# Attention, layer norm and a two-layer MLP on one core: another order for the first batch, and the second weight matrix loaded by rows

## The chip, the core and the metric

The kernel runs on one core of a Trainium2 chip. A core has five engines with instruction streams of their own: TensorE (PE) for matrix products and transposes, VectorE (DVE), ScalarE (ACT) for exponentials and other functions, GpSimd (POOL) for elementwise work, and SyncE (SP), which here only issues DMAs. DMAs are issued from the queues of SP, POOL and, at the very start, ACT. The metric is the device time of one execution in microseconds (us).

## What is computed

Eight batches with 12 heads, 448 positions and a head size of 64. Cut to what matters, the reference is

```python
q_n, k_n = rmsnorm(q, g_q), rmsnorm(k, g_k)          # over the 64 of a head
scores = (1 / 8) * q_n @ k_n^T
attn = softmax(scores)
x = (attn @ v) with the heads side by side           # 8 x 448 x 768
xn = (x - mean) / sqrt(var + 1e-6) * g_ln
out = x + relu(xn @ w_ch1) @ w_ch2                   # 768 -> 3072 -> 768
```

Inputs and output are float32; the products run in float16 with float32 sums. The first weight matrix (W1) is 768 x 3072, the second (W2) 3072 x 768. Both stay in SBUF from their load on.

## The kernel before

**Units and pairs.** Two heads make a pair, six pairs a batch. Loads and preparation go by units: the first batch has four units (one, one, two and two pairs), every later batch three units of two pairs. So units 0 to 3 are batch 0 and hold pairs 0 to 5, units 4 to 6 are batch 1, and unit 7 is the first of batch 2. For a unit, `pieces` gives the steps by a letter each: `b` takes the loaded tiles, `a` squares k and `c` squares q, `d` and `e` sum those squares, `g` (or `gk` and `gq` apart) takes the inverse root, `i` multiplies k by the product of the two gains, `j` casts k to float16 and `k` subtracts the cast from k (k is kept as a high and a low float16 part), `l` scales q, `m` doubles it, `z` brings the values.

**Which engine does what.** Some steps have tables of units that say which engine takes them: `DVE_KG` (step `i` on VectorE instead of GpSimd), `POOL_HI` (`j` on GpSimd instead of ScalarE), `POOL_DUP` (`m` on GpSimd instead of VectorE), `POOL_SQUARE` (`a` as (unit, 1) and `c` as (unit, 0) on GpSimd instead of ScalarE), `POOL_LO` (`k` on GpSimd instead of VectorE). `ACT_Q` lists the pairs whose transposed q ScalarE, not VectorE, copies from PSUM to SBUF.

**The hand-written list.** `ORDER` is a list of tokens that covers batch 0's attention, the first pair of batch 1, the normalisation of batch 0's result and the start of its first layer. `first_attention` walks it and emits each token's instructions. Every engine runs its own instructions in the order of the list, and waits only where data or buffers demand it. `K` and `Q` transpose a pair's k and q on TensorE, through PSUM, with a copy to SBUF. `Sp.i` is score block i of pair p on TensorE and the exponential of it on ScalarE; two PSUM banks take the scores in turn. `Vp.i` multiplies the exponentials with the values; after block 6, VectorE divides by the sums. `T`, `A`, `N`, `X` and `R` are the normalisation (sums, their combination, the normalised rows, their transposes, the root), `U` the first three blocks of the first layer. `L` loads a unit's inputs, `W` a third of W1, `G` the layer norm's gain. `H` and `J` with a number are fillers: that many 128-column products (`H`, L532) or transposes (`J`, L535) whose results nobody reads.

**After the list.** `run_rest` emits the MLP of each batch in chunks (L798 and L821 for the later batches, L718 and L728 for the first) and between them the attention steps of the next batch from a list that `attention` plans; a step is emitted when the MLP's estimated work has come as far as the step's share. TensorE's stream is thus an interleaving of both. Unit 7 is the first whose k and q are transposed by DMAs (`dma_k`, L306; `dma_q`, L312) issued from SP.

**W2.** `load_w2(0)` is emitted at step 47 of that plan, `load_w2(1)` at step 71, both on GpSimd's queue (L616). The DMAs convert float32 to float16. Before the second call stands a one-element cast on GpSimd (L613) that reads the transposed k of unit 7, so the call waits for that DMA transpose. Today the first call brings the left 384 columns of all 3072 rows with one DMA, the second the right 384 columns with two, of 1536 rows each. The MLP of batch 0 (`first_mlp`) has 21 chunks of the first layer and then 24 of the second (psC, L728): three tiles of 128 positions (t), two halves of the columns (g), four quarters of the 3072 rows, with six products of 128 rows each in a chunk. It runs column half by column half, in that tile by tile, in that quarter by quarter, so that one PSUM bank at a time collects a tile's 24 products before VectorE adds them (L757). The pool for these banks, `ps_m`, has three.

Of the kernel before, what the change touches and what calls it, by code (L numbers as in the profile page):

```python
# [8 lines left out]
FP32 = mybir.dt.float32  # L9
# [7 lines left out]
ts = bass.ts  # L17
# [3 lines left out]
NDC, NFF = DM // 128, FF // 128  # L21
# [3 lines left out]
PAIR_UNIT = [(u, w) for u, (_, _, m) in enumerate(UNITS) for w in range(m)]  # L25
UNIT_PAIR = [PAIR_UNIT.index((u, 0)) for u in range(len(UNITS))]
EXP_BIAS = -4.0
DVE_KG, POOL_HI, POOL_DUP, ACT_Q = (0, 6), (1, 2, 3, 4, 5, 6, *range(8, 25)), (3, 4, 5, 6), (0, 2, 4, 5)
POOL_SQUARE, POOL_LO = ((2, 1), (4, 0), (6, 0)), (5, 6)

# [1 line left out]


ORDER = """
b0 H12 a0 L4 c0 i0 e0 j0 H24 b1 gq0 d0 k0 l0 a1 m0 K0 G gk0 i1 H10 L5 c1 Q0 d1 j1 S0.0 b2 S0.1
H5 a2 e1 g1 S0.2 c2 S0.3 k1 l1 z0 d2 e2 m1 K1 S0.4 i2 H16 S0.5 S0.6 Q1 g2 H5 J8 b3 l2 j2 k2 c3
V0.0 S1.0 z2 S1.1 S1.2 V1.0 J8 a3 m2 H4 V0.1 z3 S1.3 K2 S1.4 V0.2 Q2 V0.3 V0.4 d3 S1.5 V0.5 V0.6
S2.0 S1.6 V1.1 V1.2 S2.1 e3 W0 i3 K3 V2.0 S2.2 V2.1 S2.3 Q3 j3 T0 S2.4 k3 V1.3 g3 V1.4 S2.5 S2.6  # L40
l3 b4 V1.5 m3 c4 S3.0 S3.1 V2.2 S3.2 K4 a4 V1.6 S3.3 V2.3 S3.4 Q4 d4 V2.4 V2.5 V3.0 V3.1 V3.2
V2.6 i4 S3.5 j4 J4 S3.6 V3.3 T1 K5 e4 k4 S4.0 W1 S4.1 S4.2 Q5 z4 b5 S4.3 V3.4 V4.0 V3.5 S4.4
V4.1 V4.2 S4.5 W2 V4.3 S5.0 g4 V3.6 S4.6 S5.1 J4 V5.0 V4.4 G2 S5.2 l4 T3 K6 V4.5 V5.1 V4.6 S5.3
T4 V5.2 a5 L6 V5.3 S5.4 m4 Q6 i5 S5.5 V5.4 S5.6 V5.5 V5.6 T5 S6.0 S6.1 J4 S6.2 A V6.0 S6.3 V6.1
N0 N1 S6.4 S6.5 J4 V6.2 X0 V6.3 d5 j5 N2 S6.6 V6.4 X1 z5 Q7 c5 V6.5 R U0 e5 U1 g5 X2 V6.6 M k5
U2 K7 b6 L7 a6 L8k c6 i6 l5 m5 e6 d6
""".split()
DMA_UNIT = 7
PE_SET = (DMA_UNIT + 1) % 2
# [16 lines left out]
HALF, HCOL = NFF // 2, DM // 2  # L66
# [25 lines left out]
class _Fast:  # L92
# [518 lines left out]
    def load_w2(self, g):  # L611
        if g:
            self.nc.gpsimd.tensor_copy(out=self.rr[:, DMA_UNIT:DMA_UNIT + 1],  # L613
                                       in_=self.kU[DMA_UNIT % 2][:, 0:1])
        for c in (slice(0, HALF), slice(HALF, NFF)) if g else (slice(0, NFF),):
            self.nc.gpsimd.dma_start(  # L616
                out=self.sh.w2[:, c, ts(g, 384)],
                in_=self.w2[128 * c.start:128 * c.stop, ts(g, 384)].rearrange("(c p) d -> p c d", p=128))

    def tok_tiles(self, b):  # L620
        x = self.xs[b]
# [86 lines left out]
    def first_mlp(self):  # L708

        nc, sh = self.nc, self.sh  # L710
        tiles, xnT, hT, cur = self.tok_tiles(0), self.xnT, self.hS, {}

        def up(f, i):
            if i == 0:
                cur["h"] = self.ps_m.tile([128, 512], FP32, tag="mlp", name="psH")
            ps = cur["h"]
            for dc in range(3 * i, 3 * i + 3):
                nc.tensor.matmul(ps[:, 0:384], sh.w1[:, dc, ts(f, 128)], xnT[:, dc],  # L718
                                 start=(dc == 0), stop=(dc == NDC - 1))
            if i:  # L720
                nc.scalar.activation(out=hT[:, f], in_=ps[:, 0:384], func=AFT.Relu)

        def down(t, g, s):
            if s == 0:
                cur["ps"] = self.ps_m.tile([128, 512], FP32, tag="mlp", name="psC")
            ps = cur["ps"][:, 0:HCOL]
            for f in range(3 * s, 3 * s + 3):
                nc.tensor.matmul(ps, hT[:, f, ts(t, 128)], sh.w2[:, f, ts(g, HCOL)],  # L728
                                 start=(f == 0), stop=(f == NFF - 1))
            if s == 7:  # L730
                self.add(0, t, g, ps)
                if g and t < 2:
                    self.late.append((0, t, slice(0, DM)))
                elif t == 2 and not g:
                    self.late.append((0, t, slice(0, HCOL)))
                elif t == 2:
                    self.store(0, t, slice(HCOL, DM))
            elif s == 3:
                self.store_late()

        for f in range(UP_FIRST, NFF):
            yield 6 * 384 / 2.4, [lambda f=f, i=i: up(f, i) for i in range(2)]
        for g in range(2):
            for t in range(3):
                for s in range(4):
                    yield 6 * HCOL / 2.4, [lambda t=t, g=g, s=s: down(t, g, s)
                                           for s in (2 * s, 2 * s + 1)]

    def store_late(self):
        for a in self.late:  # L750
# [500 lines left out]
```

## Time and profile before

| what | value |
|---|---|
| median of three runs | 582.78 us (581.79 to 582.78) |
| the profiled execution | 579.58 us |
| its span, first to last instruction | 578.0 us |
| TensorE, VectorE, ScalarE, GpSimd busy | 559.5, 381.7, 364.4, 207.0 us |
| fillers | 76 of L532, 32 of L535 |
| three thirds of W1, issued to landed | 14.3 us median |
| W2, first issue | 22.5 us |

The profile page gives the busy times of the engines and groups of instructions; the timeline gives start and length of each instruction and, in brackets, how long its engine had been idle before it and what ended that. Matrix products overlap in a pipeline, so a row of several has one length for all. A DMA's row in an engine's timeline is its issue; its landing is given apart. In the DMA views, q0 is GpSimd's queue and q1 the one that SP issues to.

### The profile page before, as it was taken

The numbers are of one execution on the slowest core, as the hardware profiler recorded it, in microseconds if no ns is written. First come the engines' busy times: TensorE is split into PE (matmuls) and PEld (weight loads), VectorE is DVE, ScalarE is ACT, GpSimd is POOL, SyncE is SP. The second block draws the span as 40 slices with busy tenths as digits, with TensorE's granted clock in tenths as the row PEclk, the third lists the DMA queues.
The fourth block names the chain that finished last, engine by engine and source line by source line (L and its number), as shares of the span: only waits on it lengthen the run. The fifth ranks groups of instructions, "written<-read, shape, count | busy, mean of one in ns | idle before, by whom it ended". The sixth has DMA issues, their size and how long they took to land.

```text
span 578.0 us, 13670 instructions
## 1 busy us (share of the span) xinstructions
PE 559.5 (97%) x5446; PEld 411.9 (71%) x5446; DVE 381.7 (66%) x826; ACT 364.4 (63%) x674; POOL 207.0 (36%) x224
## 2 busy tenths in 40 slices
PE   5788999999999999999999999999999999999997
PEld 4556666687686867777677768777777777878684
DVE  6989567699657586845667586854756743664424
ACT  5998787447675779557775588637777477323130
POOL 5885636404440620654241521644242320020000
PEclk9999999999999999999999999999999999999999
DMA  8999999958672876969663798958743390030201
GB/s 206 251 238 222 214 207 165 193 147 137 124 131 77 158 127 145 127 148 121 121 106 48 184 134 136 128 143 122 145 64 65 119 113 1 1 110 1 83 2 58
DMA packets 178329, 72.59 MB, mean 126 GB/s; under 512 B 138212, under 2 KB 173220, under 8 KB 178260
## 3 DMA queue, kind: packets, MB, share of 16 engines
q1 hardware_dynamic: 133876, 52.52, 44.1%
q0 software_dynamic: 43440, 18.52, 25.2%
q8 instruction: 44, 0.72, 0.5%
q10 hardware_dynamic: 944, 0.62, 0.4%
q14 instruction: 25, 0.20, 0.1%
HBM read 52.76 MB, written 11.01 MB: 110 GB/s over the span
## 4 chain that ended last, share of the span: by engine, by line
PE 77%; DVE 1%; issue 0%; DVEq 0%
PE psH L798 33%; PE psP L821 30%; PE psS L405 7%; PE oA L458 4%; PE oB L460 1%; PE psS L411 1%; DVE qn L83 0%; DVE w2s L763 0%; DVE ssq L265 0%; DVE w L763 0%; DVE xn L662 0%; DVE hS L804 0%; DVE x L475 0%; DVE xl L757 0%; DVE xl L480 0%
## 5 line engine op out<-in xcount | busy, mean ns | idle before, releaser
L421 ACT ACTIVATE E<-psS,rr_all 128x448 f16<-128x448 f32 x336 | 204.6, 634 | 47.3 <-PE psS L405 40.3
L798 PE MATMUL psH<-xnT,w 128*128 128x256 f16 (+1 forms) x2016 | 225.7, 261 | 0.0
L798 PEld LDWEIGHTS <-w 128*128 128x128 f16 x2016 | 172.8, 98 | 24.3 <-issue 4.9
L801 ACT ACTIVATE hS<-psH 128x512 f16<-128x512 f32 x150 | 89.8, 599 | 97.2 <-PE psH L798 93.0
L821 PEld LDWEIGHTS <-hS 128*128 128x128 f16 x1080 | 100.0, 98 | 57.3 <-issue 1.1
L821 PE MATMUL psP<-w,hS 128*128 128x384 f16 x672 | 127.0, 326 | 0.0
L405 PE MATMUL psS<-qU,kU 128*128 128x448 f16 x288 | 100.9, 352 | 5.0 <-ACT E L421 3.2
L458 PEld LDWEIGHTS <-E 128*128 128x128 f16 x1008 | 70.3, 98 | 35.8 <-issue 2.8
L279 POOL TENSOR_TENSOR k<-k,gprod 128x896 f32<-128x896 f32 x18 | 38.9, 2160 | 139.5 <-ACT khl L259 113.2
L804 DVE TENSOR_TENSOR hS<-hS 128x512 f16<-128x512 f16 (+1 forms) x119 | 60.2, 512 | 19.3 <-ACT hS L801 17.8
L821 PE MATMUL psP<-w2s,hS 128*128 128x384 f16 (+1 forms) x408 | 69.9, 321 | 0.0
L458 PE MATMUL oA<-v,E 128*128 128x65 f16 x864 | 66.9, 193 | 1.1 <-ACT E L421 0.6
L757 DVE SCALAR_TENSOR_TENSOR x<-psP,rs_all,x 128x384 f32<-128x384 f32 x60 | 36.4, 617 | 42.4 <-PE psP L821 41.8
L460 PE MATMUL oB<-v,E 128*128 128x65 f16 x288 | 52.0, 193 | 0.1
L832 POOL TENSOR_TENSOR x<-x,hS 128x384 f32<-128x384 f32 x21 | 23.4, 1126 | 76.1 <-ACT hS L900 75.5
L473 DVE RECIPROCAL rec_all<-oA 128x6 f32<-128x6 f32 x48 | 9.2, 193 | 53.6 <-PE oA L458 53.5
L216 POOL DMA_DIRECT2D v<-in_v_dram x54 | 41.5, 781 | 4.0 <-PE oB L460 2.7
L405 PEld LDWEIGHTS <-kU 128*128 128x128 f16 x288 | 28.0, 98 | 11.1 <-issue 2.2
L900 ACT ACTIVATE hS<-hS,rs_all 128x384 f32<-128x384 f32 x27 | 14.6, 604 | 33.0 <-DVE hS L804 33.0
L460 PEld LDWEIGHTS <-E 128*128 128x128 f16 x336 | 32.4, 96 | 0.4 <-DVE xl L480 0.3
L83 DVE SCALAR_TENSOR_TENSOR qn<-q,rr_all 128x256 f16<-128x256 f32 (+2 forms) x69 | 24.8, 420 | 7.2 <-ACT rr_all L269 7.1
L265 DVE TENSOR_REDUCE ssq<-khl 128x14 f32<-128x896 f32 (+1 forms) x24 | 25.5, 1061 | 5.0 <-ACT khl L259 4.8
(145 smaller groups left out, 616.6 us busy)
## 6 DMA issues: line engine op xcount, KB each, us to landing
k<-in_k_dram SPq DMA_DIRECT2D x19, 384.0 KB, 4.2
q<-in_q_dram SPq DMA_DIRECT2D x18, 384.0 KB, 3.9
out_dram<-x SPq DMA_DIRECT2D x14, 384.0 KB, 3.0
w<-in_moe_w_ch_dram POOLq DMA_DIRECT2D x3, 1536.0 KB, 14.3
v<-in_v_dram POOLq DMA_DIRECT2D x54, 64.0 KB, 4.4
out_dram<-x POOLq DMA_DIRECT2D x9, 384.0 KB, 2.7
w<-in_moe_w_ch_dram POOLq DMA_DIRECT2D x1, 2304.0 KB, 22.5
w<-in_moe_w_ch_dram POOLq DMA_DIRECT2D x2, 1152.0 KB, 14.4
```

Source lines behind the costliest of these rows:

```text
L216: nc.gpsimd.dma_start(out[:, :, j, 0:D], main[:, :, j])
L265: nc.vector.tensor_reduce(out=c["ssq"][:, n], in_=c["sq", n], axis=AX.X, op=ALU.add)
L279: (nc.vector if u in DVE_KG else nc.gpsimd).tensor_tensor(out=c["t"][1], in0=c["t"][1], in1=sh.gprod.unsqueeze(1).broadcast_to([128, g, D] ...
L405: nc.tensor.matmul(ps[0][:, 0:S], c["main"][:, ts(i, 128)], c["q"][:, ts(h, S)], start=True, stop=True)
L421: nc.scalar.activation(out=o, in_=x[:, 0:S], func=AFT.Exp, scale=self.units[u][3][:, g:g + 1], bias=EXP_BIAS)
L458: nc.tensor.matmul(oA[:, t, cs], E[:, ts(t, 128)], rhs, start=(i == 0 and t == 0), stop=(i == 6 and t == 2))
L460: nc.tensor.matmul(oB[:, cs], E[:, 320:448], rhs, start=(i == 0), stop=(i == 6))
L757: self.nc.vector.scalar_tensor_tensor(out=x, in0=ps, scalar=self.rs[:, b, t:t + 1], in1=x, op0=ALU.mult, op1=ALU.add)
L798: nc.tensor.matmul(ps[:, i], sh.w1[:, dc, ts(f + i, 128)], self.xnT[:, dc, 256 - N:256], start=(i == 0 and dc == 0), stop=(i == k - 1 and ...
L801: nc.scalar.activation(out=hT[:, f:f + k], in_=ps, func=AFT.Relu)
L804: nc.vector.tensor_tensor(out=out, in0=a, in1=c, op=op)
L821: nc.tensor.matmul(bank[x][:, c], a[:, f], w[:, f, c], start=(start and f == 0), stop=(stop and f == HALF - 1))
```

## The change

The tables are changed for a few units, `ORDER` is sorted anew with its fillers in other places and numbers (H: 12, 10, 7, 13, 8, 19, 11, 8, 11; J: 4, 4), W2 comes by whole rows, in four DMAs of 768 rows, two to a call, and the second layer of batch 0 runs its left column half quarter by quarter, in that tile by tile, with one PSUM bank for each of the three tiles. The right half runs as before.

By the tables, step `i` of unit 6 goes from VectorE to GpSimd; `j` of unit 1 from GpSimd to ScalarE; `m` of units 0 and 1 from VectorE to GpSimd, of unit 5 the other way; `a` of unit 5 from ScalarE to GpSimd; `k` of unit 3 from VectorE to GpSimd, of unit 6 the other way; the copy of pair 0's transposed q from ScalarE to VectorE.

```diff
-DVE_KG, POOL_HI, POOL_DUP, ACT_Q = (0, 6), (1, 2, 3, 4, 5, 6, *range(8, 25)), (3, 4, 5, 6), (0, 2, 4, 5)
-POOL_SQUARE, POOL_LO = ((2, 1), (4, 0), (6, 0)), (5, 6)
+DVE_KG, POOL_HI, POOL_DUP, ACT_Q = (0,), (2, 3, 4, 5, 6, *range(8, 25)), (0, 1, 3, 4, 6), (2, 4, 5)
+POOL_SQUARE, POOL_LO = ((2, 1), (4, 0), (5, 1), (6, 0)), (3, 5)
...
-b0 H12 a0 L4 c0 i0 e0 j0 H24 b1 gq0 d0 k0 l0 a1 m0 K0 G gk0 i1 H10 L5 c1 Q0 d1 j1 S0.0 b2 S0.1
-H5 a2 e1 g1 S0.2 c2 S0.3 k1 l1 z0 d2 e2 m1 K1 S0.4 i2 H16 S0.5 S0.6 Q1 g2 H5 J8 b3 l2 j2 k2 c3
-V0.0 S1.0 z2 S1.1 S1.2 V1.0 J8 a3 m2 H4 V0.1 z3 S1.3 K2 S1.4 V0.2 Q2 V0.3 V0.4 d3 S1.5 V0.5 V0.6
...
-T4 V5.2 a5 L6 V5.3 S5.4 m4 Q6 i5 S5.5 V5.4 S5.6 V5.5 V5.6 T5 S6.0 S6.1 J4 S6.2 A V6.0 S6.3 V6.1
-N0 N1 S6.4 S6.5 J4 V6.2 X0 V6.3 d5 j5 N2 S6.6 V6.4 X1 z5 Q7 c5 V6.5 R U0 e5 U1 g5 X2 V6.6 M k5
-U2 K7 b6 L7 a6 L8k c6 i6 l5 m5 e6 d6
+b0 a0 L4 H12 i0 c0 d0 e0 j0 k0 gk0 gq0 H10 b1 l0 c1 K0 H7 G a1 m0 L5 d1 i1 j1 Q0 e1 S0.0 g1 H13
+S0.1 k1 H8 b2 S0.2 l1 H19 a2 S0.3 S0.4 H11 d2 m1 z0 K1 c2 e2 S0.5 S0.6 g2 i2 H8 V0.0 j2 V0.1 Q1
+k2 l2 b3 c3 m2 S1.0 H11 S1.1 V0.2 z2 S1.2 V1.0 S1.3 a3 K2 S1.4 S1.5 d3 V0.3 z3 V1.1 V0.4 Q2 V0.5
...
+V4.6 L6 V5.3 a5 T4 S5.4 S5.5 S5.6 V5.4 V5.5 i5 Q6 V5.6 T5 A S6.0 S6.1 S6.2 S6.3 V6.0 V6.1 N0 J4
+V6.2 z5 N1 S6.4 d5 V6.3 S6.5 X0 N2 X1 j5 V6.4 Q7 V6.5 c5 e5 S6.6 g5 U0 X2 U1 k5 M K7 L7 b6 c6 a6
+V6.6 L8k i6 l5 e6 d6 m5 U2 R
...
-        for c in (slice(0, HALF), slice(HALF, NFF)) if g else (slice(0, NFF),):
+        for c in (0, 6) if not g else (12, 18):
             self.nc.gpsimd.dma_start(
-                out=self.sh.w2[:, c, ts(g, 384)],
-                in_=self.w2[128 * c.start:128 * c.stop, ts(g, 384)].rearrange("(c p) d -> p c d", p=128))
+                out=self.sh.w2[:, c:c + 6],
+                in_=self.w2[128 * c:128 * c + 768].rearrange("(c p) d -> p c d", p=128))
...
             if s == 0:
-                cur["ps"] = self.ps_m.tile([128, 512], FP32, tag="mlp", name="psC")
-            ps = cur["ps"][:, 0:HCOL]
+                cur[t] = self.ps_m.tile([128, 512], FP32, tag="mlp", name="psC")
+            ps = cur[t][:, 0:HCOL]
...
-        for g in range(2):
-            for t in range(3):
-                for s in range(4):
-                    yield 6 * HCOL / 2.4, [lambda t=t, g=g, s=s: down(t, g, s)
-                                           for s in (2 * s, 2 * s + 1)]
+        for g, s, t in ([(0, s, t) for s in range(4) for t in range(3)]
+                        + [(1, s, t) for t in range(3) for s in range(4)]):
+            yield 6 * HCOL / 2.4, [lambda t=t, g=g, s=s: down(t, g, s)
+                                   for s in (2 * s, 2 * s + 1)]
```

More of the change, by code (lines that the diff above doesn't have):

```diff
@@ L27 @@
 EXP_BIAS = -4.0
-DVE_KG, POOL_HI, POOL_DUP, ACT_Q = (0, 6), (1, 2, 3, 4, 5, 6, *range(8, 25)), (3, 4, 5, 6), (0, 2, 4, 5)
-POOL_SQUARE, POOL_LO = ((2, 1), (4, 0), (6, 0)), (5, 6)
+DVE_KG, POOL_HI, POOL_DUP, ACT_Q = (0,), (2, 3, 4, 5, 6, *range(8, 25)), (0, 1, 3, 4, 6), (2, 4, 5)
+POOL_SQUARE, POOL_LO = ((2, 1), (4, 0), (5, 1), (6, 0)), (3, 5)
 ORDER = """
-b0 H12 a0 L4 c0 i0 e0 j0 H24 b1 gq0 d0 k0 l0 a1 m0 K0 G gk0 i1 H10 L5 c1 Q0 d1 j1 S0.0 b2 S0.1
-H5 a2 e1 g1 S0.2 c2 S0.3 k1 l1 z0 d2 e2 m1 K1 S0.4 i2 H16 S0.5 S0.6 Q1 g2 H5 J8 b3 l2 j2 k2 c3
-V0.0 S1.0 z2 S1.1 S1.2 V1.0 J8 a3 m2 H4 V0.1 z3 S1.3 K2 S1.4 V0.2 Q2 V0.3 V0.4 d3 S1.5 V0.5 V0.6
[L40 to L43, printed above, removed]
-T4 V5.2 a5 L6 V5.3 S5.4 m4 Q6 i5 S5.5 V5.4 S5.6 V5.5 V5.6 T5 S6.0 S6.1 J4 S6.2 A V6.0 S6.3 V6.1
-N0 N1 S6.4 S6.5 J4 V6.2 X0 V6.3 d5 j5 N2 S6.6 V6.4 X1 z5 Q7 c5 V6.5 R U0 e5 U1 g5 X2 V6.6 M k5
-U2 K7 b6 L7 a6 L8k c6 i6 l5 m5 e6 d6
+b0 a0 L4 H12 i0 c0 d0 e0 j0 k0 gk0 gq0 H10 b1 l0 c1 K0 H7 G a1 m0 L5 d1 i1 j1 Q0 e1 S0.0 g1 H13
+S0.1 k1 H8 b2 S0.2 l1 H19 a2 S0.3 S0.4 H11 d2 m1 z0 K1 c2 e2 S0.5 S0.6 g2 i2 H8 V0.0 j2 V0.1 Q1
+k2 l2 b3 c3 m2 S1.0 H11 S1.1 V0.2 z2 S1.2 V1.0 S1.3 a3 K2 S1.4 S1.5 d3 V0.3 z3 V1.1 V0.4 Q2 V0.5
+V0.6 S1.6 S2.0 S2.1 W0 S2.2 e3 S2.3 V1.2 i3 V2.0 Q3 V2.1 K3 j3 k3 g3 b4 V1.3 S2.4 l3 V1.4 S2.5
+m3 S3.0 c4 S3.1 V1.5 V2.2 a4 V1.6 T0 S2.6 V2.3 K4 S3.2 S3.3 Q4 d4 V3.0 S3.4 V2.4 V2.5 V2.6 i4 e4
+V3.1 V3.2 S3.5 S4.0 S4.1 T1 j4 S3.6 J4 Q5 k4 W1 S4.2 V3.3 V4.0 S4.3 K5 V3.4 V4.1 S4.4 z4 V3.5
+V3.6 S4.5 S5.0 S5.1 b5 W2 V4.2 V4.3 g4 V5.0 T3 l4 S4.6 V4.4 V5.1 S5.2 G2 V4.5 S5.3 K6 V5.2 m4
+V4.6 L6 V5.3 a5 T4 S5.4 S5.5 S5.6 V5.4 V5.5 i5 Q6 V5.6 T5 A S6.0 S6.1 S6.2 S6.3 V6.0 V6.1 N0 J4
+V6.2 z5 N1 S6.4 d5 V6.3 S6.5 X0 N2 X1 j5 V6.4 Q7 V6.5 c5 e5 S6.6 g5 U0 X2 U1 k5 M K7 L7 b6 c6 a6
+V6.6 L8k i6 l5 e6 d6 m5 U2 R
 """.split()
```

## The prediction

> **What bounds the kernel now.** I read the page's busy times first, then the busy time in stretches of 10 us, then the timeline of each engine up to 110 us, and last the DMA queues in 2 us windows.
>
> ```profile
> span 578.0 us, 13670 instructions
> PE 559.5 (97%) x5446; PEld 411.9 (71%) x5446; DVE 381.7 (66%) x826; ACT 364.4 (63%) x674; POOL 207.0 (36%) x224
> ...
> 0.00:10.00 10.00, 5.92 (x55) 5.12 (x55) 5.42 (x17) 4.71 (x11) 4.39 (x11) 1.00 0.70 180
> 10.00:20.00 10.00, 6.04 (x70) 4.17 (x70) 9.69 (x12) 7.28 (x14) 8.42 (x10) 1.00 1.08 294
> 20.00:30.00 10.00, 8.18 (x113) 5.64 (x112) 9.16 (x14) 9.76 (x19) 7.35 (x8) 1.00 0.96 209
> 30.00:40.00 10.00, 8.38 (x116) 6.05 (x116) 8.48 (x19) 9.93 (x18) 9.22 (x10) 1.00 1.13 250
> 40.00:50.00 10.00, 8.05 (x98) 5.06 (x97) 9.61 (x29) 8.47 (x17) 4.56 (x3) 1.00 1.12 221
> 50.00:60.00 10.00, 9.58 (x126) 7.70 (x125) 9.71 (x20) 7.88 (x19) 6.38 (x6) 1.00 1.12 237
> ```
>
> The columns after the stretch are the busy times of TensorE (PE), its weight loads, VectorE (DVE), ScalarE (ACT) and GpSimd (POOL), then the granted clock, the DMA share and GB/s. TensorE is busy for 559.5 of 578.0 us, so at most 18.5 us are open. It misses 4.08 + 3.96 + 1.82 + 1.62 + 1.95 + 0.42 = 13.9 us of its time before 60 us, which is where the hand-written list runs; after that it is the bound. So the change can win only in the list, and it can lose wherever it makes TensorE wait later. In the list VectorE is full from 10 to 20 us (9.69), ScalarE from 20 to 40 (9.76, 9.93), and the DMA engines are full throughout (shares about 1.1).
>
> **The list, part by part.** The rows that carry it:
>
> ```profile
> 5.98 2.74 PE L532 MATMUL psW<-id 128*128 128x128 f16 x24
> 9.29 0.72 PE L532 MATMUL psW<-id 128*128 128x128 f16 x10
> 18.43 0.23 PE L382 MATMUL psQ<-id,qn 128*128 128x128 f16 x1 [1.41 <-DVE qn L326]
> ...
> 8.22 0.62 DVE L290 TENSOR_TENSOR khl<-w2s,khl 128x448 f16<-128x448 f32 x1
> 9.40 1.11 DVE L326 COPY qn<-qn 128x448 f16<-128x448 f16 x1
> 12.32 2.09 DVE L290 TENSOR_TENSOR khl<-w2s,khl 128x448 f16<-128x448 f32 x1 [0.20 <-POOL khl L285]
> 14.33 1.24 DVE L83 SCALAR_TENSOR_TENSOR qn<-w2s,rr_all 128x448 f16<-128x448 f32 x1
> 19.04 0.62 DVE L390 COPY qU<-psQ 128x896 f16<-128x896 f16 x1
> 54.31 0.56 DVE L706 COPY w2s<-tr 128x768 f16<-128x768 f16 x1
> ...
> 11.16 0.91 ACT L388 COPY qU<-psQ 128x896 f16<-128x896 f16 x1 [1.64 <-PE psQ L385]
> 12.51 1.16 ACT L421 ACTIVATE E<-psS,rr_all 128x448 f16<-128x448 f32 x2 [0.44 <-PE psS L405]
> 19.03 0.95 ACT L259 ACTIVATE qn<-w2s 128x896 f32<-128x896 f32 x1 [0.96 <-PE psQ L385]
> 43.11 0.94 ACT L259 ACTIVATE khl<-hS 128x896 f32<-128x896 f32 x1
> 43.95 2.02 ACT L421 ACTIVATE E<-psS,rr_all 128x448 f16<-128x448 f32 x3
> ...
> 8.81 1.55 POOL L279 TENSOR_TENSOR w2s<-w2s,gprod 128x448 f32<-128x448 f32 x1 [4.28 <-ACT khl L259]
> 12.25 1.68 POOL L257 TENSOR_TENSOR khl<-w2s 128x896 f32<-128x896 f32 x1
> 30.58 0.93 POOL L326 COPY qn<-qn 128x896 f16<-128x896 f16 x1 [2.91 <-PE oB L460]
> ```
>
> Each row gives start, length, engine, line, tiles, shapes and, in brackets, the idle time before it. Where VectorE and GpSimd meet, VectorE's work stretches: the same subtract takes 0.62 us at 8.22 and 2.09 us at 12.32, beside GpSimd's square at 12.25, and ends 0.48 after it.
>
> The first exponential (12.51) hangs on the copy of q at 9.40 (1.11 us), the transposes and ScalarE's 0.91 us copy. After the change that copy is on GpSimd (half of 0.93, so about 0.47), q's scaling comes some 0.1 later because k's root now goes first, and the copy out of PSUM is VectorE's 0.62. That makes q ready near 11.3 instead of 12.07. ScalarE, however, now also casts unit 1's k (half the width of a 0.94 us square, so 0.5 to 0.6) ahead of the first exponential, behind a GpSimd product of 1.0 to 1.55: the exponential starts near 12.0. Gain 0.5, bounds 0 and 0.9.
>
> From there to the last exponential of batch 0 (43.95 + 2.02 = 45.97) ScalarE sets the pace: 33.5 us. It loses unit 5's square (0.94 with its overlap about 0.85) to GpSimd. The other two moves, the copy that goes to VectorE and the cast that comes, lie ahead of the first exponential and are counted above. GpSimd has 2.91 us of idle time before 30.58 for what it takes over (square 1.7, two half copies 0.9; unit 3's subtract against unit 6's is a swap). If that cover is gone, its casts of k come late for the next transposes.
>
> The late transposes of pair 1's q (idle 1.41 before 18.43) leave ScalarE idle for 0.96 before 19.03. With the subtract, the scaling (1.24 against 0.62) and the copies no longer stretched in a row, pair 1's q comes 1 to 2 us sooner, and the gap goes. Against that, 19 fillers (at the 0.055 to 0.07 of the 9.29 row, over 1 us) now stand ahead of the fourth score of pair 0 and can hold its exponential by about 0.6. Net gain 0.4, bounds -0.4 and 1.0. In the remaining 25 us ScalarE's busy time (9.76, 9.93, 8.47) leaves 0.24, 0.07 and 1.53 us of its three stretches open, the last partly behind 45.97. The new order, with the lengths above, has each score's bank and each transposed k and q ready before ScalarE reaches it, but for the second half of unit 3; I take 0.6, bounds 0 and 1.2. If the stall at q goes, what is late next is unit 2's subtract, which waits for GpSimd's product and cast.
>
> The end of the list is a VectorE chain of 8.9 us, from 45.97 to the end of the copy at 54.31 (54.87): sums, normalisation, two reductions, copies. Its order is unchanged. Behind it TensorE now has pair 6's last product before the third piece of the first layer: 0.35 later. Fillers number 108 before and 107 after, so their sum is nothing; only their places count.
>
> List: -0.5 - 0.85 - 0.4 - 0.6 + 0.35 = -2.0 us, bounds +0.4 and -3.5.
>
> **W2.**
>
> ```profile
> 88.33 0.65 PE L728 MATMUL psC<-w,hS 128*128 128x384 f16 x3
> 97.58 1.14 PE L728 MATMUL psC<-w,hS 128*128 128x384 f16 x6
> 100.74 1.14 PE L728 MATMUL psC<-w,hS 128*128 128x384 f16 x6
> ...
> 61.42 1.51 POOL L616 DMA_DIRECT2D w<-in_moe_w_ch_dram  x1
> 87.33 0.18 POOL L613 CAST rr_all<-kU 128x1 f32<-128x1 f16 x1 [8.04 <-DMA kU<-khl]
> 87.57 2.09 POOL L616 DMA_DIRECT2D w<-in_moe_w_ch_dram  x2
> ...
> 80.69 2.33 SPq L306 DMA_TRANSPOSE kU<-khl  x1
> DMA to landing us min/median/max: 10.9/17.8/22.5
> ...
> DMA to landing us min/median/max: 4.0/5.6/8.0
> ...
> q0 software_dynamic: 314, 0.24, 76.7%
> q1 hardware_dynamic: 309, 0.22, 45.4%
> ...
> q0 software_dynamic: 158, 0.32, 85.7%
> q1 hardware_dynamic: 158, 0.12, 25.0%
> ...
> q0 software_dynamic: 360, 0.28, 129.9%
> ...
> q0 software_dynamic: 515, 0.39, 130.2%
> ```
>
> The landing rows are those of W2's three issues and of the transposes of k; the queue rows are packets, MB and share in 68:70, 32:34 (W1's long rows), 92:94 and 98:100. Today the first issue must land by 88.33 (61.42 + 22.5 = 83.9) and the last by about 107 (its 17.8 from 88.6 gives 106.4). Afterwards rows 1536 on are needed at the 37th product (97.58) and the last quarter at the 55th, three into the row at 100.74, so at 101.2. Landings as they are, 87.57 + 10.9 = 98.5 and 106.4, would stall TensorE by 5.2 us in all. That is the upper bound. Two things shorten it. The queues exchange packets one for one (314 against 309, 158 against 158), so a packet of twice the size takes a larger share: W1 moved 0.32 MB per window where W2 moved 0.24. W2's first half (2.36 MB) takes 7.4 such windows instead of 9.8, up to 5 us less; I take 3. It ends that much sooner, GpSimd's small value loads behind it end sooner too, and the transposes of unit 7's k, which hold the second call (6.6 us from 80.69 to 87.3; the shortest takes 4.0), land 1 to 2.6 us sooner. And alone on the engines the queue ranges from 0.28 to 0.39 MB per window: at 0.36 each quarter (1.18 MB) takes 6.6 us, and with some 2.8 us from the gate to the first packets (10.9 less 8.3 at today's mean of 0.28, and the cast) the two land 9.4 and 16.0 us behind the gate: at 94.7 and 101.3 for one 2 us earlier. I take a stall of 0.7 us, bounds 0 and 5.2; nearest is the W1 row, the only one with long packets. The fourth issue costs GpSimd another 1.0 us near 62, ahead of unit 6's cast of k; the 8.04 us that it idles before 87.33 hide it. The first product holds three PSUM banks at once, with an add of 0.6 each at its end, hidden behind interleaved scores; no matmul is added.
>
> [...] With the present rate and no earlier gate the sum would be -2.0 + 5.2 = +3.2.
>
> Sum: -2.0 + 0.7 = -1.3 us on this execution's 579.58 (span 578.0 and 1.6 around it), so 578.3. The runs shown have a median of 582.78, 3.2 above it; on that the forecast is 581.5, a gain of 0.22%.
>
> **The rivals.**
> - *The list gains and W2 is hidden:* the gate opens 2.6 us earlier and the queue holds 0.39. -2.0 to -3.5, so about 580.1. For it: bounds above; against it: full DMA engines.
> - *W2's second half comes late (slower):* packets no faster, the gate not earlier: +3.2, so 586.0. It decides once the last quarter lands over 2 us behind its need. For it speaks that the call still waits for the transposes.
> - *TensorE stays at half speed:* 24 fillers take 2.74 us (0.114 each) and the ten at 9.29 0.72, so it speeds up near 8.9 behind that busy stretch. Ten instead of 24 now stand there, with a gap of nearly 2 us after them. At 0.114 the following 47 fillers, transposes and scores take some 3 us more, of which I count 2.0 on the path: +0.7, so 583.5. [...]
> - *The sorting moves waits but gains little* because loads or GpSimd's longer share set the pace: list -0.7, W2 0.7, no change: 582.8.
>
> **How the numbers follow.** Forecast 0.34, hidden W2 0.17, late W2 0.20, half speed 0.12, no gain 0.17. What a measurement can tell is about 0.2%, or 1.2 us. The forecast itself spreads over 580.2 to 582.8. Faster takes two thirds of the forecast, the hidden case and a little of the others, 0.43; slower the late case and part of half speed, 0.30; same 0.27. The range runs from 579.4 to 586.0; the forecast's own is 580.2 to 582.8.
>
> **What would show it.** List: the last exponential of batch 0 ends near 43.6, the subtract at 12 us is no longer 2 us, the 0.96 gap is gone, the first product starts near 86.3. W2: the call leaves near 83 to 85, and TensorE waits under 1 us for a DMA near 99. The forecast is wrong if a wait for W2 of over 2 us appears, if fillers behind 10 us still take 0.11, or if VectorE's two-input work is as long as before.

## The result, and the profile after

The change made the kernel slower: 584.01 us median against 581.93 us for the kernel before on the same chip, a ratio of 1.0035, interval 1.0025 to 1.0045. That is 2.1 us more where 1.3 us less was forecast. One of the change's nine executions ran at a granted clock of 0.56 and took 976.96 us; the ratio leaves it out.

The profiled execution took 584.01 us. From the page and the busy times by stretch (us of the stretch, then busy time of TensorE, its weight loads, VectorE, ScalarE and GpSimd, granted clock, DMA share, GB/s):

```profile
span 582.5 us, 13666 instructions
PE 560.8 (96%) x5445; PEld 413.3 (71%) x5445; DVE 380.3 (65%) x825; ACT 363.2 (62%) x673; POOL 210.4 (36%) x227
...
0.00:10.00 10.00, 3.98 (x31) 3.34 (x32) 4.89 (x16) 4.47 (x11) 3.26 (x11) 1.00 0.77 185
10.00:20.00 10.00, 9.28 (x106) 7.97 (x103) 6.06 (x9) 5.89 (x12) 8.32 (x10) 1.00 1.13 298
20.00:30.00 10.00, 7.50 (x101) 5.10 (x99) 8.66 (x14) 9.57 (x19) 9.60 (x10) 1.00 1.03 249
```

The stretch from 10 to 20 us has turned over. VectorE's busy time there fell from 9.69 to 6.06 us. In part that is stretched work that is gone (the subtract that took 2.09 us at 12.32 takes 0.93 at 12.87); in part VectorE now waits, for 2.88 us in front of 18.57, for TensorE. ScalarE's busy time fell too, from 7.28 to 5.89, and ScalarE sets the pace later; TensorE's rose from 6.04 to 9.28. TensorE's timeline of the change shows why:

```profile
5.54 1.25 PE L532 MATMUL psW<-id 128*128 128x128 f16 x10
9.34 0.29 PE L368 MATMUL tr<-id,khl 128*128 128x128 f16 x1 [2.55 <-DVE khl L290]
9.42 0.85 PE L371 MATMUL tr<-id,khl 128*128 128x128 f16 x6
10.91 0.85 PE L385 MATMUL psQ<-id,qn 128*128 128x128 f16 x6
12.48 0.53 PE L405 MATMUL psS<-qU,kU 128*128 128x448 f16 x1 [0.72 <-DVE qU L390]
12.80 1.59 PE L532 MATMUL psW<-id 128*128 128x128 f16 x13
15.79 1.36 PE L532 MATMUL psW<-id 128*128 128x128 f16 x19
18.03 0.50 PE L371 MATMUL tr<-id,khl 128*128 128x128 f16 x6
...
103.75 0.65 PE L728 MATMUL psC<-w,hS 128*128 128x384 f16 x3 [0.98 <-DMA w<-in_moe_w_ch_dram]
```

Ten fillers, then 2.55 us of idle time, and TensorE works at half speed until it speeds up within the row at 15.79: six transposes take 0.85 us where those at 18.03 take 0.50, and 13 fillers take 1.59. The fillers at half speed stand in front of the scores of pair 0, and ScalarE waits in front of each of the first four. The granted clock reads 1.00 in this stretch all the same; the lengths of the rows show the speed better here. The last row is the wait for W2's last quarter.

ScalarE's timeline of the change:

```profile
13.05 0.63 ACT L421 ACTIVATE E<-psS,rr_all 128x448 f16<-128x448 f32 x1 [0.76 <-PE psS L405]
14.81 0.63 ACT L421 ACTIVATE E<-psS,rr_all 128x448 f16<-128x448 f32 x1 [0.77 <-PE psS L405]
16.03 0.63 ACT L421 ACTIVATE E<-psS,rr_all 128x448 f16<-128x448 f32 x1 [0.59 <-PE psS L405]
17.38 1.16 ACT L421 ACTIVATE E<-psS,rr_all 128x448 f16<-128x448 f32 x2 [0.71 <-PE psS L405]
20.93 0.95 ACT L259 ACTIVATE qn<-w2s 128x896 f32<-128x896 f32 x1
21.78 0.62 ACT L421 ACTIVATE E<-psS,rr_all 128x448 f16<-128x448 f32 x1
...
30.19 2.23 ACT L421 ACTIVATE E<-psS,rr_all 128x448 f16<-128x448 f32 x4 [0.45 <-PE psS L405]
45.17 1.90 ACT L421 ACTIVATE E<-psS,rr_all 128x448 f16<-128x448 f32 x3 [0.58 <-PE psS L405]
```

Pair 1's first exponential starts at 21.78; before it was 20.12, right behind the square at 19.03. Of that, 0.45 us is older than the list: ScalarE's first square of k waits for its load and starts at 6.46, before at 6.01. Batch 0's last exponential ends at 47.07 (45.97 before), and the first psC starts at 89.70 (88.33).

Much later both timelines run in parallel. TensorE's row of 24 psP products, before and after:

```profile
507.20 4.06 PE L821 MATMUL psP<-w2s,hS 128*128 128x384 f16 x24
```

```profile
509.80 4.06 PE L820 MATMUL psP<-w2s,hS 128*128 128x384 f16 x24
```

2.60 us apart: 1.37 at the first psC (0.45 the load of k, 0.92 the list), 0.98 from the wait for W2, 0.25 elsewhere. The remaining 1.8 us between the two profiled executions (584.01 and 579.58) lies behind this row, in the last stores. From this row to the end of the span it is 70.8 us in the trace of before and 71.9 to 72.8 us in all others, also where nothing near the end differs, so it is taken as the execution's and not the change's. Below I therefore compare landmarks ahead of this row, and times over many executions.

### The profile page after: what moved, and what is told of

It reads as the page before. It is cut to its first block, busy times and chain, and to the rows that moved or that the text cites. A ratio compares the mean times of both kernels' runs of the same rounds, so it can differ in the third digit from the quotient of the medians.

```text
span 582.5 us, 13666 instructions
## 1 busy us (share of the span) xinstructions
PE 560.8 (96%) x5445; PEld 413.3 (71%) x5445; DVE 380.3 (65%) x825; ACT 363.2 (62%) x673; POOL 210.4 (36%) x227
## 4 chain that ended last, share of the span: by engine, by line
PE 83%; DMA 8%; ACT 4%; DVE 2%; SPq 1%; issue 1%; POOL 0%; DVEq 0%; ACTq 0%
PE psH L797 34%; PE psP L820 30%; PE psS L405 7%; PE oA L458 5%; DMA w<-in_moe_w_ch_dram 3%; PE psC L728 3%; ACT E L421 3%; DMA k<-in_k_dram 2%; PE oB L460 2%; PE psS L411 2%; DMA w2s<-in_k_dram 1%; SPq L154 1%; DMA hS<-in_q_dram 1%; DMA kU<-khl 1%; SPq L146 1%
## 5 line engine op out<-in xcount | busy, mean ns | idle before, releaser
L279 POOL TENSOR_TENSOR k<-k,gprod 128x896 f32<-128x896 f32 x19 | 41.0, 2157 | 142.7 <-ACT khl L259 99.2
```

The source lines that it names most:

```text
L279: (nc.vector if u in DVE_KG else nc.gpsimd).tensor_tensor(out=c["t"][1], in0=c["t"][1], in1=sh.gprod.unsqueeze(1).broadcast_to([128, g, D] ...
```

## The experiments

Landmarks of the main traces in us: start of the first exponential, of pair 1's first exponential and of the first psC; TensorE's waits for W2 in the first product; start of the row of 24; and the ratio of the times to the kernel before, each time on the same chip.

| kernel | first exp | pair 1 | psC | wait | row of 24 | ratio |
|---|---|---|---|---|---|---|
| before | 12.51 | 20.12 | 88.33 | 0 | 507.20 | 1 |
| the change | 13.05 | 21.78 | 89.70 | 0.98 | 509.80 | 1.0035 |
| list_only | 12.73 | 21.21 | 89.19 | 0 | 508.74 | 1.0024 |
| w2_only | 12.38 | 19.99 | 88.21 | 3.45 | 512.67 | 1.0073 |
| quarters_only | 12.98 | 20.47 | 88.70 | 0 | 507.96 | 0.9996 |
| before_h10 | 13.64 | 20.57 | 88.79 | 0 | 508.25 | 1.0004 |
| after_h24 | 11.87 | 19.08 | 87.42 | 2.54 | 509.22 | 1.0037 |
| list_h24 | 12.29 | 19.50 | 87.92 | 0 | 507.57 | 0.9992 |
| list_h24_few | 11.99 | 19.02 | 87.57 | 0 | 506.45 | 0.9988 |

Single executions differ by when the first loads land: the first exponential moves by up to 0.6 us between kernels that are alike there (before, w2_only, quarters_only). Much of that goes when the landmarks are counted from ScalarE's first square of k, which waits for its load (5.88 to 6.52 us). The first psC then stands 82.32 us behind it in before, 82.33 in w2_only and before_h10, 82.56 in quarters_only; 83.24 and 83.04 in the change and list_only; 81.41, 81.40 and 81.35 in after_h24, list_h24 and list_h24_few. Between the first psC and the row of 24, traces without a wait for W2 still differ by up to 0.8 us (418.87 in before, 418.88 in list_h24_few, 419.46 in before_h10, 419.65 in list_h24).

**The change's two halves apart.** list_only is the change with the two W2 edits taken back, w2_only the kernel before with only those two.

```diff
 list_only, against the change:
-        for c in (0, 6) if not g else (12, 18):
+        for c in (slice(0, HALF), slice(HALF, NFF)) if g else (slice(0, NFF),):
...
-        for g, s, t in ([(0, s, t) for s in range(4) for t in range(3)]
-                        + [(1, s, t) for t in range(3) for s in range(4)]):
+        for g in range(2):
+            for t in range(3):
+                for s in range(4):
```

> New tables and new list, W2 loaded and multiplied as before. Clock theory (ten fillers instead of 24 leave TensorE at half speed until about 16 us, and the late scores of pair 0 cost the list about 1.4 us): +1.0 to +1.7 us on the kernel before, with the gaps of 0.6 to 0.8 us ahead of the first exponentials as in the changed kernel, and no wait for W2. Rival, the order theory (the new order is slower by itself, the speed of TensorE is a side effect): the same here. If the two halves of the change are independent, this and the W2 half alone add up to the whole, +2.1 to +2.6 us.

> Old tables and old list, W2 by rows and its first product by row quarters. W2 theory (the last quarter lands about 1 us behind its need, since the second call still waits for the transposes of unit 7): TensorE waits 0.7 to 2.0 us for a DMA near 100 us, +0.7 to +2.0 us. Rival (the wait in the changed kernel comes from the late list): no wait, 0 to +0.3 us.

Measured: list_only 583.09 us against 581.78, ratio 1.0024 (1.001 to 1.0038); no wait for W2, psC 0.86 later. So the new list alone loses, and the old W2 load carries its later psC without a stall. w2_only 586.65 us against 581.78, ratio 1.0073 (1.005 to 1.0097): far more than the 0.7 to 2.0 us expected. By the ratios the halves alone would add up to 5.6 us, and the change has 2.1, so they are not independent. TensorE's timeline of w2_only:

```profile
98.02 1.14 PE L728 MATMUL psC<-w,hS 128*128 128x384 f16 x6 [0.40 <-DMA w<-in_moe_w_ch_dram]
...
104.88 0.65 PE L728 MATMUL psC<-w,hS 128*128 128x384 f16 x3 [3.05 <-DMA q<-in_q_dram]
105.89 1.15 PE L728 MATMUL psC<-w,hS 128*128 128x384 f16 x3
107.44 1.95 PE L728 MATMUL psC<-w,hS 128*128 128x384 f16 x6
109.54 0.65 PE L728 MATMUL psC<-w,hS 128*128 128x384 f16 x3
```

and its busy times by stretch, with the granted clock third from the right:

```profile
102.00:104.00 2.00, 0.00 (x0) 0.00 (x0) 0.00 (x0) 0.01 (x1) 0.00 (x0) 1.00 1.15 231
104.00:106.00 2.00, 1.12 (x13) 0.83 (x13) 0.00 (x0) 0.25 (x1) 0.00 (x0) 0.92 1.47 215
106.00:108.00 2.00, 2.00 (x12) 1.00 (x10) 0.62 (x1) 0.94 (x2) 0.00 (x0) 0.50 1.52 193
108.00:110.00 2.00, 2.00 (x13) 1.11 (x12) 0.57 (x1) 0.46 (x2) 0.00 (x0) 0.73 1.45 181
110.00:112.00 2.00, 2.00 (x21) 1.27 (x19) 0.74 (x3) 1.84 (x4) 0.03 (x1) 1.00 0.25 55
```

The wait of 3.05 us stands at the 55th product, the first that needs the last quarter (the releaser named is a load that landed at the same time; in the other three traces with such a wait it is W2). Behind it the granted clock falls to 0.50 and three products take 1.15 us instead of 0.65. The offset to the trace of before grows from -0.1 us ahead of the waits to 5.3 behind them: 3.45 of waits and some 2.0 of slow clock.

**The first product's order alone.** quarters_only is the kernel before with the row quarters and the three banks, but W2's old load.

```diff
-        for g in range(2):
-            for t in range(3):
-                for s in range(4):
+        for g, s, t in ([(0, s, t) for s in range(4) for t in range(3)]
+                        + [(1, s, t) for t in range(3) for s in range(4)]):
```

> The list and W2's load as before the change, only the first product in row quarters over three banks. If the order of the product costs nothing by itself: no difference, 0 +- 0.3 us, no wait at psC. If three open banks or the later first sums cost something (the first addition leaves 8 us later, the up products' banks are short): 0.5 us or more slower, to be seen as a wait at psC or psH between 88 and 110 us.

581.9 against 581.68 us by the medians, ratio 0.9996 (0.9986 to 1.0006), no wait at psC. With the old load the order costs nothing that this can show; what costs in w2_only is the load by rows.

**The fillers ahead of the second batch's first step.** after_h24 is the change with 24 fillers where it has ten, before_h10 the kernel before with ten where it has 24.

```diff
 after_h24:
-... gk0 gq0 H10 b1 ...
+... gk0 gq0 H24 b1 ...
 before_h10:
-... j0 H24 b1 ...
+... j0 H10 b1 ...
```

> The changed kernel with its ten fillers behind the first small product made 24 again, as many as before; nothing else. Clock theory: TensorE is at full speed for the first transposes (seven of them within 0.5 us instead of 0.85), the gaps ahead of the first exponentials fall under 0.3 us each, the first exponential of pair 1 comes near 19.5 instead of 21.8, and the whole is 1.5 to 2.5 us shorter than the changed kernel, so -0.4 to +0.8 us on the kernel before. Order theory: the transposes speed up but the gaps stay, and it stays at +1.5 to +2.5 us.

> The kernel before with its 24 fillers made ten; nothing else. Clock theory: TensorE stays at half speed behind them, and pair 0's scores come late: +1.0 to +2.5 us. Order theory: under +0.4 us, since the old order does not hang on TensorE there.

TensorE's timeline of after_h24:

```profile
5.52 2.74 PE L532 MATMUL psW<-id 128*128 128x128 f16 x24
8.88 0.29 PE L368 MATMUL tr<-id,khl 128*128 128x128 f16 x1 [0.62 <-DVE khl L290]
10.18 0.50 PE L385 MATMUL psQ<-id,qn 128*128 128x128 f16 x6
11.67 0.89 PE L532 MATMUL psW<-id 128*128 128x128 f16 x13
...
99.84 0.65 PE L728 MATMUL psC<-w,hS 128*128 128x384 f16 x3
103.03 0.65 PE L728 MATMUL psC<-w,hS 128*128 128x384 f16 x3 [2.54 <-DMA w<-in_moe_w_ch_dram]
```

The fillers take up the idle time in front of the transposes (0.62 left of 2.55), TensorE is at full speed from 10 us on (0.50 for six, 0.89 for 13), and pair 1 starts 2.7 us sooner than in the change, psC 2.28 sooner (1.83 counted from k's square). The half speed is shown as the cause of the list's loss. But the time stays, ratio 1.0037 (1.0015 to 1.0058), where the clock theory had 1.5 to 2.5 us less than the change: the wait for W2 grew from 0.98 to 2.54, because W2's last quarter came only 0.72 us sooner. In this trace the granted clock stayed at 1.00 behind the wait. It is of one of the short executions (582.68 us, of 582.07 to 587.95); whether the long ones lost the clock behind the wait, as w2_only did, was not traced.

before_h10 shows the same half speed (transposes 0.85 for six up to 15.3 us), yet pair 1 and psC come only 0.45 us later, as much as k's square does (6.46 against 6.01), and in time it costs nothing measurable, 1.0004 (0.9989 to 1.0019); the clock theory had +1.0 to +2.5 us. So half speed alone does not cost it. The old list has only five fillers between the first four scores where the new one has 13, 8 and 19. That these fillers make the difference is the likely reading; ten warm-up fillers with few fillers behind them were not run.

**The list without the W2 edits, at full speed.** list_h24 is list_only with 24 fillers.

> The new tables and list with 24 fillers in place of ten ahead of the second batch's first step, and W2 loaded as before the change. Clock theory: TensorE is at full speed by the first products, the first exponential starts near 11.9 us and that of pair 1 near 19.1 (before: 12.51 and 20.12), the first psC starts near 87.4 (before: 88.33), and there is no wait for W2 of the kind that took 2.54 us with the row load. 0.9 us earlier from there on: 0.9 us faster than before, ratio 0.9985. Rival, that the list's gain is lost further on whatever W2 does (the new list alone stood 0.86 us behind the kernel before at the first psC but 1.3 at its end): no difference, 0 to +0.4 us.

580.94 against 581.68 us, ratio 0.9992 (0.9983 to 1.0002): psC 0.41 earlier and no wait for W2. It lies between the two expectations, and a gain is not proven. Against list_only (1.0024) it shows in the times what the half speed costs: some 1.9 us. What it settles is how little the list gains behind pair 1's first exponential: from there to the first psC the table gives 68.2 us for every kernel with the old list (20.12 to 88.33, 19.99 to 88.21, 20.47 to 88.70, 20.57 to 88.79) and, in all kernels with the new one in which no work is done twice, 67.9 to 68.6.

**What bounds the list behind that point.** Two kernels on list_h24, one with two exponentials of pair 2 done twice on ScalarE, one with a sum of squares done twice on VectorE.

```diff
 list_h24_act:
-            nc.scalar.activation(out=o, in_=x[:, 0:S], func=AFT.Exp,
+            for _ in range(2 if p == 2 and i in (1, 3) else 1):
+                nc.scalar.activation(out=o, in_=x[:, 0:S], func=AFT.Exp,
 list_h24_dve:
-            nc.vector.tensor_reduce(out=c["ssq"][:, n], in_=c["sq", n], axis=AX.X, op=ALU.add)
+            for _ in range(2 if (u, n) == (3, 1) else 1):
+                nc.vector.tensor_reduce(out=c["ssq"][:, n], in_=c["sq", n], axis=AX.X, op=ALU.add)
```

> The list with 24 fillers and W2 as before, with two of pair 2's exponentials done twice on ScalarE (the second writes the same numbers again). From the start of pair 1's first exponential to the first psC all traces so far show 67.9 to 68.4 us, whatever the list or the fillers. Theory that ScalarE's own work bounds the list from there on (19.1 to 19.7 us busy of the 20 from 20 to 40): the two exponentials lie on the path, and this stretch grows from 68.4 to 69.5 (two times 0.53 to 0.58), the time by 1.1 us against the list with 24 fillers. Rival (the waits between engines or the path over VectorE and GpSimd bound it): the stretch stays within 0.3 of 68.4.

> The list with 24 fillers and W2 as before, with the sum of unit 3's squares of k done twice on VectorE (1.08 us near 23 us, the same numbers again). Theory that ScalarE bounds the list: VectorE is up to 95% busy but not last, the stretch from pair 1's first exponential to the first psC stays within 0.4 of 68.4 us. Rival (VectorE, whose stretched operations the new list was to shorten, bounds it): the stretch grows by 0.8 to 1.1 us, to 69.2 or more.

Neither settles it as planned. With the two exponentials the stretch to the first psC is 68.70, 0.28 more than in list_h24: expected was 69.5, and the rival's bound was 68.7. The time is 581.17 against 581.59 us, ratio 1.0009 (0.9994 to 1.0023). The last group of batch 0's exponentials starts at 43.26 in list_h24 and at 43.90 here; less the 0.22 by which this execution was later at pair 1, that is 0.42 of the 1.06 us put in; the wait of 0.45 us at 27.91 and the one of 0.16 at 39.56 that ScalarE has in list_h24 are gone, as these rows of list_h24_act show for the first of them, the second row having no wait in it:

```profile
24.48 4.14 ACT L422 ACTIVATE E<-psS,rr_all 128x448 f16<-128x448 f32 x7
28.90 2.21 ACT L422 ACTIVATE E<-psS,rr_all 128x448 f16<-128x448 f32 x4
```

By this one trace ScalarE has about 0.6 us of slack here and becomes the bound beyond that. With the sum doubled on VectorE the same group starts 23.80 us behind pair 1's first exponential (43.31 less 19.51), in list_h24 23.76: up to there VectorE is not the bound. The first psC of that trace is 2.0 us late for another reason, so the expected stretch to psC cannot be read from it. Its GpSimd timeline:

```profile
59.63 1.68 POOL L257 TENSOR_TENSOR qn<-q 128x896 f32<-128x896 f32 x1 [4.72 <-DMA w2s<-in_k_dram]
```

In list_h24 this square starts at 54.92 without a wait; here it stood 4.72 us behind a load, and TensorE later waited 1.76 us at 64.46 for a copy that followed from it. The times (581.25 us, 0.9996, 0.9981 to 1.001) hold no such delay on the median, so it belongs to some executions; whether the doubled sum makes it likelier is open.

**Fewer fillers between the scores.** list_h24_few is list_h24 with the seven groups behind the 24 cut from 77 to 30.

> The list with 24 fillers ahead of the second batch's first step and W2 as before, and the seven groups of fillers behind it cut from 77 matmuls to 30 (7, 13, 8, 19, 11, 8, 11 to 4, 4, 4, 6, 4, 4, 4). If the fillers between the first products hold them up: ScalarE's wait of 0.62 us in front of 15.09 goes, pair 1's first exponential starts 0.3 to 0.6 us sooner, and the time is 581.0 - 0.5, the ratio to the kernel before 0.998 to 0.9985. If they lie beside the exponentials: no change, 0.999 to 1.0. If the clock falls without them, TensorE's products between 12 and 18 us take twice as long and pair 1's first exponential starts 0.5 us or more later.

580.95 against 581.59 us, ratio 0.9988 (0.9979 to 0.9997): 0.7 us faster than the kernel before, the one version that beats both. From the first exponential to pair 1's it takes 7.03 us against 7.21 in list_h24, and the wait of 0.62 us fell to 0.38: less than the 0.3 to 0.6 us expected. Against list_h24 (0.9992) a gain is not shown. The busy times by stretch of list_h24_few:

```profile
10.00:20.00 10.00, 7.38 (x74) 5.42 (x75) 8.06 (x11) 7.95 (x16) 8.71 (x11) 0.83 1.10 299
```

ScalarE is busier than in the change (7.95 against 5.89) although the granted clock fell to 0.83, so this spell of slow clock cost little.

**W2's gate.** after_nogate is the change without the one-element cast; after_h24_3and1 is after_h24 with three of the four pieces in the early call, run twice.

```diff
 after_nogate:
-        if g:
-            self.nc.gpsimd.tensor_copy(out=self.rr[:, DMA_UNIT:DMA_UNIT + 1],
-                                       in_=self.kU[DMA_UNIT % 2][:, 0:1])
 after_h24_3and1:
-        for c in (0, 6) if not g else (12, 18):
+        for c in (0, 6, 12) if not g else (18,):
```

> The change as it is, without the small GpSimd copy that holds the second W2 call until the transposes of unit 7's k have landed. W2 theory: the call leaves 5.5 us sooner (GpSimd sat 5.55 us idle in front of the copy), the fourth piece lands near 98 instead of 103.7, and the wait of 0.98 us goes: 1.0 us faster than the change, 1.1 us slower than before (ratio 1.002). Rival: the transposes then share the transfer engines with W2's packets and land later than the 4.1 us they took; what waits for them moves by more than 1 us, and it is no faster than the change, or slower.

587.36 against 581.68 us, ratio 1.0096 (1.0081 to 1.0111): the rival was right. The call left at 81.29 and no wait for W2 remained, but the transposes of unit 7 now came behind it, from 82.70 on. SP's and TensorE's timelines of after_nogate:

```profile
82.70 8.93 SPq L306 DMA_TRANSPOSE kU<-khl  x1
91.74 7.04 SPq L312 DMA_TRANSPOSE qU<-qn  x3
```

```profile
105.20 0.35 PE L405 MATMUL psS<-qU,kU 128*128 128x448 f16 x1 [2.48 <-DMA qU<-qn]
```

Their issue took 8.93 and 7.04 us (1.67 and 4.07 in the change), TensorE waited 2.48 us for q, and the granted clock fell behind that to 0.62 (106 to 108 us) and 0.53 (108 to 110). Some 0.65 us of the loss against the change stands ahead of the call: pair 1's first exponential is at 22.43 in this trace, behind a longer spell at half speed.

> The change with 24 fillers, and three of W2's four pieces in the early call, one behind the gate. W2 theory: the fourth piece is late only because it queues behind the third one after the gate; alone it lands some 9 us behind the gate, near 95, before its product at 100.5, and the wait of 2.54 us is gone: first psC near 87.4, no wait behind it, 0.9 us faster than before, ratio 0.9985. Rival: 0.59 MB more in the early call delay the loads and transposes of the second batch's unit 7 and the steps behind them, and the first psC moves later by 1 us or more; then it is 0 to 2 us slower than before.

> The change with 24 fillers and three W2 pieces early, once more. Its first profile showed no wait for W2 and a first psC at 87.84, but its executions ran from 580.5 to 585.4 us, with the profiled one among the fastest. If the early third piece pushes the transposes of unit 7 (in the first profile the transposes of its k took 6.2 us to issue, against 1.7 in the change) to the edge of their need, slower executions show a wait of TensorE for them of 1 to 3 us between 95 and 110 us, with the granted clock below 1 behind it, and the median stays at 582.5 to 584. If the spread came from the chip of that job alone, the median is 580.5 to 581.5 and no such wait appears.

583.11 against 581.68 us the first time (1.0023, 1.0008 to 1.0038), 583.65 against 581.84 the second (1.0031, 0.9999 to 1.0063), each spread over some 5 us. The first profile caught a short execution (580.56) without a wait for W2, the second a middle one (583.44). GpSimd and TensorE in the second:

```profile
58.46 2.57 POOL L616 DMA_DIRECT2D w<-in_moe_w_ch_dram  x3
93.34 0.18 POOL L613 CAST rr_all<-kU 128x1 f32<-128x1 f16 x1 [14.55 <-DMA kU<-khl]
```

```profile
103.31 0.65 PE L728 MATMUL psC<-w,hS 128*128 128x384 f16 x3 [2.46 <-DMA w<-in_moe_w_ch_dram]
```

With the early third piece the transposes take longer (issue 8.35 us here, 6.19 in the first, 2.74 in after_h24), so the gate opens at 93.34 instead of 85.42. The last piece then lands 9.7 us behind its call, as expected, but the call is 7.9 us later. The wait is W2's again, not the transposes' as I had expected; the median lies where that expectation had it all the same.

## Why the prediction was wrong

**The half speed was a rival, and it turned the list's gain into a loss.** It had a chance of 0.12 and a price of 2.0 us on the path; the sum itself put the fillers at nothing ("their sum is nothing; only their places count"). Counted from k's square, ten instead of 24 fillers cost 1.83 us at the first psC (the change against after_h24) and 1.64 (list_only against list_h24). The mechanism and nearly the price held; what was wrong was the chance, for the trace of before had both facts in it (fillers of 0.114 us in the row of 24 and of 0.072 in the ten behind it, and k's transposes not ready before 8.89, which leaves a gap behind ten), and with "fillers behind 10 us still take 0.11" its own sign was named: 13 of them took 1.59 us. Ten fillers (1.25 us) and a gap of 2.55 us were followed by long rows in the change, 24 fillers (2.74 us) and a gap of 0.62 by short ones from 10 us on in after_h24. From 9.34 us on TensorE worked in the change for some 6.4 us, with one gap of 0.72 in front of 12.48, until its rows were short; the runs do not show why it took that long. Without this loss the rest of the forecast can be read from after_h24 and list_h24.

**Term by term for the list, by after_h24 and list_h24 against before.**
- First exponential, -0.5: measured -0.64 in after_h24 and -0.73 in list_h24 (5.86 and 5.77 us behind k's square, 6.50 before). Right, a little better. The subtract at 12 us was shorter, as forecast: 1.40 us in after_h24, 0.93 in the change.
- Gap at pair 1's q, -0.4: from the first exponential to pair 1's 7.21 us against 7.61, so -0.40. Right.
- Unit 5's square, -0.85, and small waits, -0.6: wrong. From pair 1's first exponential to batch 0's last, list_h24 takes 25.66 us (19.50 to 45.16), before 25.85. The square of 0.94 is gone from ScalarE, but the waits in this stretch are 0.45 + 0.16 + 0.58 = 1.19 us where before had 0.42. The step that failed is "the new order has each score's bank and each transposed k and q ready before ScalarE reaches it": it has not, by 0.77 us more than before. -1.45 forecast, -0.19 measured.
- Tail, +0.35: from that end to the first psC 42.76 against 42.36, so +0.4. The size is right.

ScalarE's rows with a wait between pair 1's first exponential and batch 0's last, first before, then list_h24:

```profile
42.58 0.63 ACT L421 ACTIVATE E<-psS,rr_all 128x448 f16<-128x448 f32 x1 [0.42 <-PE psS L405]
```

```profile
27.91 2.23 ACT L421 ACTIVATE E<-psS,rr_all 128x448 f16<-128x448 f32 x4 [0.45 <-PE psS L405]
...
39.56 0.63 ACT L421 ACTIVATE E<-psS,rr_all 128x448 f16<-128x448 f32 x1 [0.16 <-PE psS L405]
...
43.26 1.90 ACT L421 ACTIVATE E<-psS,rr_all 128x448 f16<-128x448 f32 x3 [0.58 <-PE psS L405]
```

In sum, counted from k's square, the list gives -0.9 us at psC with 24 fillers (after_h24 and list_h24 alike) and +0.7 (list_only) to +0.9 (the change) with ten, where -2.0 was forecast. The bounds of that sum were written as +0.4 and -3.5; its terms as listed add up to -0.1 and -3.6.

**W2, +0.7.** The wait of 0.98 us looks right and is so by luck, out of two errors. The last quarter was to land 16.0 us behind the gate's opening; its product started 17.5, 17.6 and 17.9 us behind it (86.25, 85.42, 86.96 to 103.75, 103.03, 104.88 in the change, after_h24 and w2_only). The gate in GpSimd's timeline, in the change and in after_h24:

```profile
86.25 0.18 POOL L613 CAST rr_all<-kU 128x1 f32<-128x1 f16 x1 [5.55 <-DMA kU<-khl]
```

```profile
85.42 0.18 POOL L613 CAST rr_all<-kU 128x1 f32<-128x1 f16 x1 [7.00 <-DMA kU<-khl]
```

That product would stand 13.1 us behind the first psC without a wait (99.84 + 0.65 less 87.42). So the wait is 4.4 us less the distance from gate to psC: 3.45 us in the change, 2.0 in after_h24, 1.25 in w2_only give 1.0, 2.4 and 3.2, measured 0.98, 2.54 and 3.05. The distance of 3.45 was so large because the list was late. With the list at full speed (after_h24) the wait was 2.54 us, over the 2 us which the forecast named as its refutation. The mis-sized term is the landing, by 1.5 us: from 88 to 102 us of the change GpSimd's queue moved 2.29 of the 2.36 MB, a mean of 0.33 MB in 2 us where 0.36 was assumed (0.25 in 96:98, where the other queue sent 170 packets beside its 167), and the rest fell into 102:104, where the two sent 477 and 483 packets. The gate came at 86.25, where the call was to leave near 83 to 85. The longer rows did bring what was counted on earlier: in 68:70 the queue moved 0.29 MB (before 0.24), packet for packet with the other one (198 each; before 314 and 309). The rival of a late W2 thus held in w2_only and after_h24, with 5.4 us of waits and slow clock in the one and a wait of 2.54 us in the other.

**What it did not see:** that the two halves of the change work against each other. In after_h24 the first psC came 2.28 us sooner than in the change, and the wait for W2 took back 1.56 of it, since the gate opened only 0.83 sooner: the transposes that it waits for were issued 2.27 us sooner (79.79 against 82.06) but opened the gate 5.63 us behind their issue instead of 4.19. And the gate cannot simply go: in after_nogate, with W2's call 1.41 us ahead of them, the transposes of k took 8.93 us to issue instead of 1.67.

## What to carry to other kernels

Judge warm-up fillers by the rows behind them, and read the speed from the lengths of like rows: behind ten fillers and 2.55 us of idle time six transposes took 0.85 us in the change; behind 24 and 0.62 us they took 0.71 in after_h24, and 0.50 from 10.18 on. Where work stays at half speed, the fillers in front of needed products take twice as long too (13 took 1.59 us in the change, 0.89 in after_h24). A list that ends earlier is worth only what the next deadline allows (2.28 us at psC in after_h24 against the change, of which the wait for W2 took back 1.56), so set the landing of the next weights against the new start before counting a gain. And freeing a busy engine does not shorten the chain if waits of a few tenths come in its place (0.94 us off ScalarE in list_h24, and 0.77 us more of waits): count the waits of the whole stretch, not only the one removed.

## What the runs showed of the chip

After a single wait in the middle of dense work, TensorE's granted clock fell to about half for some 3 us in two traces and did not in two others. Waits of 2.46 us (after_h24_3and1_again) and 2.54 us (after_h24) left the granted clock at 1.00; waits of 2.48 us (after_nogate) and 3.05 us (w2_only) were followed by 0.50 to 0.62, and in w2_only by some 2.0 us of extra time. So the length alone does not decide near 2.5 us; what else does, these traces do not show.

Between 10 and 16 us of the change the rows show half speed (six transposes 0.85 us at 10.91, 0.50 at 18.03) while the granted clock reads 1.00; behind the waits near 105 us the granted clock shows it (0.50 to 0.73 from 106 to 110 us). Whether the early stretch is only not recorded is open.

Where VectorE and GpSimd meet, VectorE's work still stretches, here from 1.09 to 2.73 us. The same scaling of q from VectorE's timelines, and GpSimd's product beside it, first in list_h24:

```profile
56.87 2.73 DVE L83 SCALAR_TENSOR_TENSOR qn<-hS,rr_all 128x896 f16<-128x896 f32 x1
...
56.56 2.08 POOL L279 TENSOR_TENSOR k<-k,gprod 128x896 f32<-128x896 f32 x1
```

and then in list_h24_dve, where GpSimd was waiting for a load at that time:

```profile
56.81 1.09 DVE L83 SCALAR_TENSOR_TENSOR qn<-hS,rr_all 128x896 f16<-128x896 f32 x1
```

1.64 us for one meeting. The new list shortened such meetings in the first 20 us (the subtract at 12 us from 2.09 to 0.93), and did not end them.
